# w_phi on Sync's queue, a GpSimd copy ahead of unit 1's loads, and a new table of order

## Chip, cores and metric

The kernel runs on one core of a Trainium2 chip (trn2). The metric is device time in microseconds (us) for one execution. Before the change three runs took 286.98, 287.28 and 287.29 us, median 287.28.

## What is computed

A linear attention whose feature map is a pair of exponentials, and behind it a feed-forward layer with a maximum over three projections. Its inputs are q, k, v of 8 batches x 8 heads x 576 positions x 64, `w_phi` of 64x128, and four weights of the feed-forward layer.

```python
def phi(x):
    proj = einsum('bhsd,df->bhsf', x, w_phi)
    proj = proj - max(abs(proj), axis=-1)
    return concatenate([exp(proj), exp(-proj)], axis=-1)
q_p, k_p = phi(q), phi(k)
kv  = einsum('bhsf,bhsd->bhfd', k_p, v);  z = sum(k_p, axis=2)
x   = einsum('bhsf,bhfd->bhsd', q_p, kv) / (einsum('bhsf,bhf->bhs', q_p, z) + 1e-6)
h   = maximum(maximum(x @ w1, x @ w2), x @ w3)     # x as 4608 x 512
out = h @ w_out
```

## The kernel before, in words

The attention is cut into 16 units of 4 heads (two pairs of heads). The feed-forward layer is cut into 9 chunks of 512 tokens; chunk b needs units 2b and 2b+1, the last chunk needs all of them.

What one unit does, with the names that the trace shows (lines of the kernel before):

- Load. Units 0 to 3 go by TensorE transposes (`by_pe`). Unit 0's q and k come as four float32 pieces on Sync's (SP's) queue, one piece per pair of heads (L447), and are cast to bf16 by L451 on ACT or DVE. Units 1 to 3 come on GpSimd's (POOL's) queue, cast on the way (L458). From unit 4 on, q and k come as float32 on SP or POOL (L472) and POOL casts them (L476). v is float32 in `v_raw` (L472).
- T: the transposes `tps<-ident,qk_bf`, L490 for unit 0 and L493 for units 1 to 3, evacuated by DVE into `qkT` (L496). Later units use a DMA transpose (L508).
- G: the projections `psq` and `psk` from `qkT` and `w2` (L535, L530), 18 tiles in groups of four and a last one of two. DVE takes the absolute maxima (`mqp`, `mk`, L554), ACT the exponentials of the keys (`Ek`, L548).
- M: the queries once more, the other way round, with the maxima subtracted: `psm` by L616 and L619 for units 0 and 1 (this needs all of the unit's `mqp`, and the tile `minus`), by L614 later, where the maxima reach `qkT` through a small DMA `qkT<-mT` (L570). ACT takes `Eq` from it (L627).
- V and K: POOL multiplies v with `em` into `vab` (L589); K, the sum over positions, is `kvps` (L643, 72 matmuls).
- N and x: the numerators and denominators `psn` (L661), divided by DVE (L667, L668) into `x_sb`, and turned into `xT` (L681, L684, or the DMA transpose L691).

A chunk then runs the products `ups` (L714), their maximum (`hT`, L720 to L724), the products into `ops` (L742, L747), the copy into `osb` (L755) and the store (L762). While the attention of the first units runs, the weights are turned and multiplied (`pwT` L797, `pm` L811) and subtracted on POOL (L785).

What sets the order: every piece of work is a node with a number, its engine may be one of several, and a table of words (`PLAN`) gives for each node the engine, the buffer slots and a start by which the nodes are sorted. Each engine runs its instructions strictly in that order; semaphores do the waiting. Only the sequence counts on the chip: an instruction whose input is late holds all that stands behind it on its engine. `fill` puts matmuls on a constant tile (`idler`, L842) into gaps that the table leaves on TensorE in the first part of the program; they only keep TensorE busy.

Around the change: `w_phi` comes as two DMAs of 64 rows on ACT's queue (L360) ahead of ACT's table load, and DVE casts it in three pieces (L405, L406) before the first `qkT` copy (L496). The v loads of units 1, 2 and 3 are held back by a one-element copy on DVE (L467) that reads a unit's `qkT` and writes into the tile to be loaded. TensorE starts with 17 idlers.

## Time and profile before

The profiled execution took 285.3 us from its first to its last instruction; the page shows no other time of that execution. The median of the runs is 287.28 us, so 1.98 us lie around the span.

| what | before |
|---|---|
| median of 3 runs | 287.28 us |
| profiled execution, its span | 285.3 us |
| busy: TensorE matmul, DVE, ACT, POOL | 274.8, 208.4, 192.5, 125.0 us |
| idlers (L842), 28 of them | 9.5 us of TensorE's busy time |
| first matmul that is work (`tps` L490) | at 6.50 us |
| first `ups` of a chunk | at 42.86 us |
| last copy before the last store | at 281.95 us |
| chain that ended last | PE 81%, DMA 8%, ACT 6% |

How to read it: TensorE is shown busy nearly throughout, but at the start a part of that is idlers, and a busy share there says nothing of progress. Rows of the timeline give start, length, engine, line, operation and, in brackets, how long the engine had been idle before it and what ended that. Rows of the windows view give a stretch, its length and each engine's busy time in it.

### The profile page before, as it was taken

The page shows a single profiled execution, that of the slowest core. Times are in us where ns is not written, and L with a number is a line of the kernel's source. Part 1 is how long each engine was busy: PE and PEld are TensorE (multiplying, and loading weights), DVE is VectorE, ACT ScalarE, POOL GpSimd, SP SyncE. Part 2 cuts the span into 40 slices and gives each one's busy share as a digit, 9 for nine tenths or more (in the row PEclk, how much of TensorE's full clock was granted, in tenths as well). Part 3 has the DMA queues.
Part 4 walks back from the last instruction along what each step waited for, and adds up shares of the span by engine and source line. Part 5 has one row for each costly group of instructions (what it writes and reads, how often), then busy time and mean ns, then how long its engine had stood idle before and what let it go on. Part 6 is the DMA issues. An engine that isn't in the chain of part 4 may idle for free.

```text
span 285.3 us, 8441 instructions
## 1 busy us (share of the span) xinstructions
PE 274.8 (96%) x3485; PEld 155.7 (55%) x3522; DVE 208.4 (73%) x442; ACT 192.5 (67%) x445; POOL 125.0 (44%) x107
## 2 busy tenths in 40 slices
PE   8889999999999999999999999999999999999995
PEld 3557674565565555456565565555544664444442
DVE  2897899988999868688678779987975472227431
ACT  3798979997999987878868887779775400041001
POOL 9338999945923574417534950160080501000000
PEclk9997999999999999999999999999999999999999
DMA  7999979999899998988897998294420134153135
GB/s 192 203 284 262 312 144 305 341 239 250 221 293 196 225 232 280 251 156 202 258 251 272 268 199 182 99 182 81 82 62 3 27 54 90 37 110 76 37 85 173
DMA packets 67760, 51.46 MB, mean 180 GB/s; under 512 B 48778, under 2 KB 53002, under 8 KB 67722
## 3 DMA queue, kind: packets, MB, share of 16 engines
q1 hardware_dynamic: 62734, 43.38, 60.6%
q0 software_dynamic: 4576, 7.28, 12.1%
q8 instruction: 27, 0.44, 0.6%
q10 hardware_dynamic: 412, 0.28, 0.3%
q14 instruction: 11, 0.09, 0.1%
HBM read 34.67 MB, written 9.44 MB: 155 GB/s over the span
## 4 chain that ended last, share of the span: by engine, by line
PE 81%; DMA 8%; ACT 6%; POOL 1%; DVE 1%; issue 1%; ACTq 0%; POOLq 0%
PE ups L714 29%; PE ops L747 15%; PE ops L742 10%; PE psn L661 6%; PE kvps L643 6%; DMA qk_bf<-in_q_dram 5%; PE psm L614 5%; PE psq L535 4%; DMA qkT<-mT 3%; ACT Eq L627 3%; PE pm L811 2%; ACT Ek L548 2%; PE tps L493 1%; PE psq L530 1%; POOL qk_bf L458 1%
## 5 line engine op out<-in xcount | busy, mean ns | idle before, releaser
L714 PE MATMUL ups<-xT,w_bf 128*128 128x512 bf16 x415 | 101.5, 379 | 1.4 <-ACT Ek L548 0.5
L627 ACT ACTIVATE Eq<-psm 128x512 bf16<-128x512 f32 (+1 forms) x160 | 81.9, 582 | 15.6 <-PE psm L614 12.8
L589 POOL TENSOR_TENSOR vab<-v_raw,em 128x1152 bf16<-128x1152 f32 (+1 forms) x36 | 68.1, 1907 | 36.8 <-ACT em L585 27.9
L548 ACT ACTIVATE Ek<-psk 128x512 bf16<-128x512 f32 x128 | 73.5, 622 | 8.5 <-PE psk L535 5.8
L714 PEld LDWEIGHTS <-w_bf 128*128 128x128 bf16 x432 | 40.6, 98 | 45.4 <-issue 1.0
L720 DVE TENSOR_TENSOR hT<-hT,ups 128x512 bf16<-128x512 bf16 x54 | 36.4, 683 | 24.6 <-ACT hT L722 13.6
L554 DVE TENSOR_REDUCE mqp<-psq 128x4 bf16<-128x512 f32 (+1 forms) x80 | 49.0, 633 | 5.1 <-PE psk L535 2.9
L747 PE MATMUL ops<-wout_bf,hT 128*128 128x512 bf16 (+2 forms) x215 | 51.5, 373 | 0.5 <-issue 0.2
L554 DVE TENSOR_REDUCE mk<-psk 128x4 f32<-128x512 f32 x64 | 43.0, 683 | 0.7 <-PE psk L535 0.5
L747 PEld LDWEIGHTS <-hT 128*128 128x128 bf16 x222 | 21.1, 98 | 23.1
L668 DVE TENSOR_TENSOR x_sb<-psn,rden 128x320 bf16<-128x320 f32 x64 | 31.5, 492 | 2.2
L722 ACT ACTIVATE hT<-ups 128x512 bf16<-128x512 f32 x31 | 18.5, 615 | 21.1 <-PE ups L714 21.0
L755 ACT COPY osb<-ops 128x512 f32<-128x512 f32 (+2 forms) x17 | 9.6, 581 | 30.2 <-PE ops L747 12.7
L661 PEld LDWEIGHTS <-Eq 128*128 128x128 bf16 x640 | 24.9, 97 | 8.0
L755 DVE COPY osb<-ops 128x512 f32<-128x512 f32 x20 | 13.6, 689 | 20.1 <-PE ops L747 18.5
L661 PE MATMUL psn<-kv_sb,Eq 128*128 128x65 bf16 x640 | 26.8, 194 | 0.1
L742 PE MATMUL ops<-xT 128*128 128x512 bf16 x88 | 24.2, 379 | 0.4
L614 PE MATMUL psm<-qkT,wphi_m 128*128 128x512 bf16 (+1 forms) x70 | 22.3, 359 | 0.7 <-DMA qkT<-mT 0.6
L535 PE MATMUL psq<-w,qkT 64*128 64x128 bf16 x256 | 21.5, 217 | 0.5 <-DVE qkT L496 0.2
L476 POOL CAST qk_bf<-q_raw 128x1152 bf16<-128x1152 f32 x12 | 13.8, 1148 | 18.1 <-DMA q_raw<-in_q_dram 9.7
L535 PE MATMUL psk<-w,qkT 64*128 64x128 bf16 x256 | 21.3, 217 | 0.4 <-DVE mqp L554 0.4
L535 PEld LDWEIGHTS <-qkT 64*128 64x128 bf16 x512 | 14.8, 94 | 10.7 <-issue 8.1
(76 smaller groups left out, 272.6 us busy)
## 6 DMA issues: line engine op xcount, KB each, us to landing
out_dram<-osb SPq DMA_DIRECT2D x64, 128.0 KB, 2.5
v_raw<-in_v_dram SPq DMA_DIRECT2D x14, 576.0 KB
k_raw<-in_k_dram SPq DMA_DIRECT2D x11, 576.0 KB, 4.9
q_raw<-in_q_dram SPq DMA_DIRECT2D x11, 576.0 KB, 4.9
w_bf<-in_moe_w_dram POOLq DMA_DIRECT2D x3, 768.0 KB, 11.1
v_raw<-in_v_dram POOLq DMA_DIRECT2D x2, 576.0 KB, 13.7
qk_bf<-in_k_dram POOLq DMA_DIRECT2D x3, 288.0 KB, 13.4
qk_bf<-in_q_dram POOLq DMA_DIRECT2D x3, 288.0 KB, 13.6
```

The costliest lines, as they stand in the source:

```text
L535: nc.tensor.matmul(ps()[:, i, :], lhsT=cols[r, :], rhs=w2[r, c, :], start=True, stop=True)
L548: nc.scalar.activation(Ek[s]()[:, tiles_of(t0, n), :], of(1), EXP, scale=1.0 - 2.0 * s)
L554: nc.vector.tensor_reduce((mq, mk)[c]()[:, tiles_of(t0, n)], of(c), AXX, ALU.max, apply_absolute_value=True)
L589: (nc.vector if n_.eng == "DVE" else nc.gpsimd).tensor_tensor(vab()[:, g, t0:t1, 0:D], vb()[:, t0:t1, :], em()[:, g, t0:t1].unsqueeze(2).t ...
L614: nc.tensor.matmul(psm()[:, 0:w], lhsT=wphi_m, rhs=rhs, start=True, stop=True)
L627: nc.scalar.activation(Eqb()[s][:, cols], psm()[:, 0:w], EXP, scale=1.0 - 2.0 * s)
L661: nc.tensor.matmul(psn()[:, c, :], lhsT=Eqb()[g][:, t0:t0 + P], rhs=kv()[:, pr, ab, g, :], start=(g == 0), stop=(g == 1))
L668: nc.vector.tensor_tensor(x_sb()[:, pr, :, ab, :], psn()[:, :, 0:D], rden().to_broadcast([P, 5, D]), ALU.mult)
L714: nc.tensor.matmul(ups(), lhsT=w_bf[i + 1][:, ct, j * P:(j + 1) * P], rhs=tokens_of(ct), start=(ct == 0), stop=(ct == CT - 1))
L720: nc.vector.tensor_tensor(hT()[:, j, :], hT()[:, j, :], ups(), ALU.max)
L742: nc.tensor.matmul(ops_()[:, 0:width], lhsT=tile_of(ct, tt), rhs=line_w[c_i > MOVE][:, ct, cols], start=(ct == 0), stop=False)
L747: nc.tensor.matmul(ops_()[:, 0:width], lhsT=hT()[:, j, tt * P:(tt + 1) * P], rhs=wout_bf[:, j, cols], start=False, stop=(j == JT - 1))
```

## The change

1. `w_phi` is one DMA on SP's queue, whose source is read twice (a leading dimension of two with step 0), and stands between unit 0's pieces; ACT issues none.
2. The copies on DVE that held the v loads of units 1 to 3 (L467) are gone. In their place a one-element copy on POOL reads `k_raw` of unit 0 and writes into the tile that unit 1's q or k is to be loaded into, so that these two loads, and all that stands behind them on POOL, are issued only after that piece of unit 0's k is there.
3. `fill` leaves a wider margin ahead of a matmul in the first 10 us; TensorE has 17 idlers instead of 28, and 9 instead of 17 at its start.
4. Some buffers are no longer named by nodes that only come before their use (G, M, K and N). This does not change what an instruction reads or writes.
5. The whole table `PLAN` is another.

```diff
-GATES = (None, (0, 0), (1, 0), (2, 0))
+HOLD = (1, 0)
...
-0G@0.7 4A@0.7 6S0@0.7 2D0@0.8 3D@1.0 10S0@1.2 1G@1.3 12S@1.6 85G0@1.9 8S@2.1 84G@2.6 1075G@3.3 158G1@4.0 5D@4.1
+0G@0.7 2D0@0.7 12S0@0.7 3D@0.8 8S0@1.1 4S@1.6 10S@2.0 6S@2.5 14S0@3.0 13A0@3.4 9D@4.5 5D@4.9 17T1@5.0 18D0@5.7 11A@5.8
...
-        while gap > (0.35 if t < WARM else 0.5) and t < n.start - 0.2:
+        while gap > (0.35 if t < WARM else 0.5) and t < n.start - (0.45 if t < 10 else 0.2):
...
-    for ab in range(2):
-        nc.scalar.dma_start(wphi_f[ab * D:(ab + 1) * D, :], w_phi)
...
-    n_phi = node("phi", 0, {"ACT": 1.2}, lambda: None, [], [], pipe=0.05, lat=2.0, dmas=2)
+    n_phi = node("phi", 0, {"SP": 1.2}, lambda: nc.sync.dma_start(wphi_f, w_phi.unsqueeze(0).to_broadcast([2, D, DF])), [], [],
+                 pipe=0.05, lat=2.0)
...
+                        if (what, i) == HOLD:
+                            first.append((n_.deps[0], raw))
...
+                    held = []
+                    if u == 1:
+                        land, src = first[0]
+                        held.append(nd("gate", {"POOL": 0.1}, lambda what=what, src=src: nc.gpsimd.tensor_copy(
+                            qk()[0:1, what, 0, 0:1], src()[0:1, 0, 0:1]), [land], [src, qk]))
...
-                if by_pe and u < len(GATES) and GATES[u]:
-                    src, col = units[GATES[u][0]]["qkT"], BATCHES[GATES[u][1]][0] * P
-                    gates.append(nd("gate", {"DVE": 0.1}, lambda src=src, col=col, raw=raw: nc.vector.tensor_copy(
-                        raw()[0:1, 0, 0:1], src()[0:1, col:col + 1]), [], [src, raw]))
```

Three places show what the table does at the start. First SP, from its first load on, before the change:

```order
L447 DMA q_raw<-in_q_dram 128x576
L447 DMA k_raw<-in_k_dram 128x576 x2
L447 DMA q_raw<-in_q_dram 128x576
L472 DMA v_raw<-in_v_dram 128x2x576 x2
L570 DMA qkT<-mT 1x18x128
```

SP at the same place with the change:

```order
L441 DMA k_raw<-in_k_dram 128x576
L441 DMA q_raw<-in_q_dram 128x576
L407 DMA wphi_f<-in_w_phi_dram 128x1x128
L441 DMA k_raw<-in_k_dram 128x576
L441 DMA q_raw<-in_q_dram 128x576
L468 DMA v_raw<-in_v_dram 128x2x576
L563 DMA qkT<-mT 1x18x128
```

`w_phi` now stands third, ahead of the second pieces of k and q; unit 0's v is the sixth load, where it stood on POOL's queue before, and the two held v loads of later units are gone from SP's start.

Second POOL, from the identity tile on, before the change (the DMA rows are loads that POOL issues; `qk_bf` of units 1 and 2, then v of unit 0 and two weights):

```order
masks.py:199 AFFINE_SELECT ident<-ident 128x128
L409 TENSOR_SCALAR minus<-ident 128x128
L458 DMA qk_bf<-in_k_dram 128x2x576
L458 DMA qk_bf<-in_q_dram 128x2x576
L419 DMA w_bf<-in_moe_w_dram 128x4x768
L458 DMA qk_bf<-in_k_dram 128x2x576
L458 DMA qk_bf<-in_q_dram 128x2x576
L472 DMA v_raw<-in_v_dram 128x2x576
L419 DMA wout_bf<-in_moe_w_out_dram 128x6x512
L419 DMA w_bf<-in_moe_w_dram 128x4x768
```

POOL at the same place with the change:

```order
masks.py:199 AFFINE_SELECT ident<-ident 128x128
L458 CAST qk_bf<-k_raw 1x1 x2
L454 DMA qk_bf<-in_q_dram 128x2x576
L454 DMA qk_bf<-in_k_dram 128x2x576
L413 DMA w_bf<-in_moe_w_dram 128x4x768
L454 DMA qk_bf<-in_q_dram 128x2x576
L402 TENSOR_SCALAR minus<-ident 128x128
L454 DMA qk_bf<-in_k_dram 128x2x576
L468 DMA v_raw<-in_v_dram 128x2x576
L413 DMA wout_bf<-in_moe_w_out_dram 128x6x512
L413 DMA w_bf<-in_moe_w_dram 128x4x768
L582 TENSOR_TENSOR vab<-v_raw,em 128x9x64 x2
```

The two copies of one element stand ahead of every load; the copies wait for unit 0's second piece of k, the fourth DMA on SP. `minus` has moved behind four loads, the v in this list is unit 1's, and the first two products `vab` follow the last load.

Third ACT, from the last casts or exponentials of unit 0's keys on, before the change (`Ek_208` and `Ek_222` are unit 0's two halves, `Eq_0` its queries):

```order
L548 ACTIVATE Ek_208<-psk 128x512 x2
L548 ACTIVATE Ek_222<-psk 128x512
L548 ACTIVATE Ek_208<-psq 128x2x128
L627 ACTIVATE Eq_0_75<-psm 128x512
L627 ACTIVATE Eq_0_76<-psm 128x512
L548 ACTIVATE Ek_222<-psq 128x2x128
```

ACT with the change (`Ek_172` and `Ek_211` are unit 0's, `Ek_330` and `Ek_347` unit 1's):

```order
L541 ACTIVATE Ek_172<-psk 128x512
L578 ACTIVATE em<-mk 128x9 x2
L541 ACTIVATE Ek_211<-psq 128x2x128
L541 ACTIVATE Ek_211<-psk 128x512
L620 ACTIVATE Eq_0_73<-psm 128x512
L620 ACTIVATE Eq_0_74<-psm 128x512
L541 ACTIVATE Ek_330<-psk 128x512
L541 ACTIVATE Ek_347<-psk 128x512
```

All ten exponentials of unit 0's keys and two of `em` now stand ahead of the first `Eq`. On TensorE the first `psm` that it reads has moved too: with the change it stands behind the first half of unit 1's transposes (16 matmuls, L489), and unit 0's projections all stand ahead of these.

309 lines of the change are left out of this document (151 added, 158 removed).

## The prediction

> **What bounds the kernel now.** I read the page's busy line first, then the windows by stage, then the timeline of the start.
>
> ```profile
> PE 274.8 (96%) x3485; PEld 155.7 (55%) x3522; DVE 208.4 (73%) x442; ACT 192.5 (67%) x445; POOL 125.0 (44%) x107
> L842 PE MATMUL idler<-idle 128*128 128x512 bf16 x28 | 9.5, 462 | 1.0 <-DVE idle L412 1.0
> ```
>
> TensorE is busy for 274.8 of 285.3 us, but 9.5 us of it are idlers. The stretches say where it is really the bound (columns: length; busy time of PE, PEld, DVE, ACT, POOL; granted clock; share of the DMA engines; GB/s):
>
> ```profile
> 10.00:24.00 14.00, 12.33 (x197) 8.83 (x199) 13.23 (x28) 12.77 (x32) 6.41 (x9) 0.91 1.17 247
> 24.00:43.00 19.00, 18.75 (x411) 13.72 (x412) 16.48 (x40) 16.67 (x43) 17.69 (x15) 0.98 0.97 242
> 43.00:60.00 17.00, 16.90 (x206) 9.18 (x207) 16.61 (x33) 16.93 (x40) 16.95 (x11) 1.00 1.05 301
> 60.00:110.00 50.00, 49.14 (x802) 29.19 (x810) 43.52 (x96) 45.08 (x108) 24.82 (x17) 1.00 1.00 241
> 110.00:180.00 70.00, 68.50 (x964) 39.31 (x968) 56.56 (x119) 56.48 (x133) 34.30 (x26) 1.00 0.90 233
> 180.00:282.00 102.00, 101.24 (x883) 52.20 (x891) 58.15 (x115) 40.10 (x90) 17.18 (x16) 1.00 0.35 76
> ```
>
> From 43 us on TensorE idles 0.10 + 0.86 + 1.50 + 0.76 = 3.22 us in 239: it is the bound, and a new order can win at most about that. Between 10 and 43 us DVE and ACT are as full as TensorE (ACT idles 1.23 + 2.33 = 3.56 us, DVE 0.77 + 2.52), the DMA engines are full too, and TensorE fills up with idlers. So the head goes at the pace of ACT's and DVE's streams, and what counts is when they start and where they stop. Their start:
>
> ```profile
> 0.73 1.25 ACTq L360 DMA_DIRECT2D wphi_f<-in_w_phi_dram  x2
> 0.73 0.40 SPq L447 DMA_DIRECT2D q_raw<-in_q_dram  x1
> 1.04 5.52 PE L842 MATMUL idler<-idle 128*128 128x512 bf16 x17 [1.04 <-DVE idle L412]
> 3.53 0.67 ACT L451 CAST qk_bf<-q_raw 128x576 bf16<-128x576 f32 x1 [0.24 <-DMA q_raw<-in_q_dram]
> 4.64 0.67 ACT L451 CAST qk_bf<-k_raw 128x576 bf16<-128x576 f32 x1 [0.44 <-DMA k_raw<-in_k_dram]
> 6.11 0.41 DVE L405 CAST w<-wphi_f 64x128 bf16<-64x128 f32 x1 [2.14 <-DMA wphi_f<-in_w_phi_dram]
> 6.50 0.61 PE L490 MATMUL tps<-ident,qk_bf 128*128 128x128 bf16 x8
> 6.54 0.22 DVE L406 CAST wphi_m<-wphi_f 64x128 bf16<-64x128 f32 x1
> 7.14 0.69 DVE L496 COPY qkT<-tps 128x1024 bf16<-128x1024 bf16 x1 [0.39 <-PE tps L490]
> 7.64 0.67 ACT L451 CAST qk_bf<-k_raw 128x576 bf16<-128x576 f32 x1 [2.33 <-DMA k_raw<-in_k_dram]
> 7.89 0.23 PE L535 MATMUL psq<-w,qkT 64*128 64x128 bf16 x1
> 9.29 0.67 ACT L451 CAST qk_bf<-q_raw 128x576 bf16<-128x576 f32 x1 [0.98 <-DMA q_raw<-in_q_dram]
> 9.87 4.14 ACT L548 ACTIVATE Ek<-psk 128x512 bf16<-128x512 f32 x8
> 12.07 1.24 PE L493 MATMUL tps<-ident,qk_bf 128*64 128x128 bf16 x32
> 13.47 0.38 PE L616 MATMUL psm<-qkT,w 128*128 128x512 bf16 x1
> 13.87 0.42 ACT L548 ACTIVATE Ek<-psq 128x256 bf16<-128x256 f32 x1
> 14.13 1.13 ACT L627 ACTIVATE Eq<-psm 128x512 bf16<-128x512 f32 x2
> 15.44 3.08 ACT L627 ACTIVATE Eq<-psm 128x512 bf16<-128x512 f32 x6
> ```
>
> The four pieces of unit 0 land at 3.53, 4.64, 7.64 and 9.29 us: 1.11 us apart at first, later 3.0 and 1.65, since other loads share the engines. The first projection is at 7.89 us, and ACT's stream of exponentials begins at 9.87 us, once it has cast the last piece; unit 1 is transposed at 12.07 us.
>
> **The change part by part.** The sum is made against the span of 285.3 us; the median of the runs, 287.28 us, is 1.98 us more, and I add the difference in span to it.
>
> *Fewer idlers.* Seventeen ended at 1.04 + 5.52 = 6.56 us and held the first transposes, whose casts were done at 4.64 + 0.67 = 5.31 us. At the 0.43 us from one to the next at which they begin, nine end by 4.9. That frees up to 1.2 us, but the first projection needs `w_phi` as well, so its landing decides.
>
> *w_phi between the pieces.* What it costs there is the largest unknown. ACT's queue is q10 on the page:
>
> ```profile
> q10 hardware_dynamic: 412, 0.28, 0.3%
> ```
>
> 0.3% of 16 engines for 285.3 us is 13.7 us of one engine for 412 packets, 33 ns each. The 128 rows of `w_phi` are 4.3 us of one engine: 0.27 us if 16 engines share them, 4.3 if one has them all, and what stands behind them on those engines waits for that. The source counts 2 x 64 x 128, and I take two engines, 2.1 us. Behind the second piece (4.64) this puts `w_phi` at some 6.4 us, between 6.7 and the 6.11 at which its second half landed before, and so much later than its size suggests.
> The Trainium skill has a rule that speaks against this edit ("DMA: Bandwidth & Descriptors", the section on why a DMA increments its semaphore by 16): the number of engines is the largest up to 16 that divides the slowest dimension of both sides, so a leading broadcast of two would leave two engines. No row here shows that for this DMA; by it the term is my 2.1 us, and without it 0.27.
>
> With `w_phi` at 6.4, DVE's three casts (0.41 + 0.22 + less than 0.41, partly overlapped, 0.65 as between 6.11 and 6.76) end at 7.05, the copy of `qkT` at 7.7, and the first projection is at about 7.75 instead of 7.89. The second k lands a piece later, 6.4 + 1.1 = 7.5 (before 7.64), the second q at 8.6 (9.29): nothing else competes by then. ACT's stream begins behind its cast at 9.25 instead of 9.87, 0.6 earlier. It gains nothing else: the first q's cast has gone to DVE, where 0.68 us of an f32 copy lies in the wait for `w_phi`, and the 1.25 us of issuing on ACT lay ahead of a table load that nothing waited for.
>
> *The hold.* Two copies of one element, then the loads.
>
> ```profile
> L467 DVE CAST v_raw<-qkT 1x1 f32<-1x1 bf16 x3 | 0.4, 134 | 0.0
> 1.90 0.94 POOL L458 DMA_DIRECT2D qk_bf<-in_k_dram  x1
> 9.72 0.72 POOL L472 DMA_DIRECT2D k_raw<-in_k_dram  x1 [1.65 <-DMA qk_bf<-in_k_dram]
> 11.12 0.73 POOL L472 DMA_DIRECT2D q_raw<-in_q_dram  x1 [0.68 <-DMA qk_bf<-in_q_dram]
> 18.41 0.51 ACT L585 ACTIVATE em<-mk 128x9 f32<-128x9 f32 x4
> 20.46 4.49 POOL L589 TENSOR_TENSOR vab<-v_raw,em 128x576 bf16<-128x576 f32 x4 [1.21 <-DMA v_raw<-in_v_dram]
> 26.09 1.27 PE L643 MATMUL kvps<-vab,Ek 64*128 64x65 bf16 x72
> 42.86 2.54 PE L714 MATMUL ups<-xT,w_bf 128*128 128x512 bf16 x11
> ```
>
> A copy takes 0.13 us on DVE; on POOL I take 0.3 for both. So unit 1's first load is issued at 7.5 + 0.3 = 7.8 us instead of 1.90, and behind it on POOL wait two weights, unit 2's q and k, `minus` (needed with the first `psm`, long after) and unit 1's v. Before, the two landed by 9.72 and 11.12, 7.8 and 9.2 us after that first issue, against unit 0's pieces. Now only v of unit 0 is in their way. Lower bound: the issue 0.94, the 1.7 us that a piece on SP takes beside its own 1.1 (0.73 to 3.53), and twice the 1.40 from 9.72 to 11.12: 5.4 us, 13.2. Upper bound: 9.2 us again, 17.0. I take 14.5, nearer to the lower end since the pieces are gone: 2.4 us after 12.07.
>
> What waits for that: TensorE runs unit 1's first transposes ahead of unit 0's first `psm`. ACT has, from 9.25 on, eight exponentials (4.14), two short ones of 0.42 and two `em` of 0.51 / 4, 5.25 us, to 14.5. The first `Eq` can start at 14.5 + 0.62 (half of the 1.24) + 0.66 (a `psm` at 13.47, its `Eq` at 14.13), 15.8: ACT stops for 1.3 us. Before, the same content without the two `Eq` that stood among it was done by 15.44 - 1.13 + 0.26 = 14.6. So the head is 1.2 us behind at this place.
>
> *Given back later.* Unit 0's v is now the sixth load on SP, 8.6 + 2 x 1.1 = 10.8 us, instead of the release at 20.46; POOL can multiply as soon as its issues end, at about 14.5. K of unit 0 (26.09 us before), the numerators and unit 0's x follow earlier, and with them there is work for ACT and DVE where ACT idled 2.33 us between 24 and 43 us. I count all of that: 1.2 - 2.3 = -1.1 for the head, the first `ups` at 41.8. Ends: -3.5 (no stop, all idling gone) and +2.5 (a long stop, little regained).
>
> *The rest of the table.* From 43 us on 3.22 us can be won, and a bad order can lose as much. One row shows what an order does:
>
> ```profile
> 112.22 1.54 ACTq L570 DMA_DIRECT2D qkT<-mT  x1
> ```
>
> The small DMA of the maxima, issued by ACT, held ACT's queue for 1.54 us; three of four such issues move to SP. I take a third of the bound, -1.1, ends -3.2 and +2. At the end the last copy moves from ACT (0.48 us at 281.95) to DVE, within 0.2; nothing.
>
> ```profile
> 281.95 0.48 ACT L755 COPY osb<-ops 128x384 f32<-128x384 f32 x1 [1.40 <-PE ops L747]
> ```
>
> Sum: -1.1 - 1.1 = -2.2 us, a span of 283.1 and a time of **285.1 us**.
>
> **The rivals.**
>
> *w_phi costs nothing* (0.27 us): it lands by 4.9, k at 6.0, q at 7.1; ACT starts at 7.75, 2.1 earlier, unit 1 lands at 13.0, and ACT stops from 13.0 to 14.3: a lead of 1.6 at the stop, of 0.3 behind it. Then -0.3 - 2.3 for the head and -1.1 for the rest: 283.6 us. For it: 64 KB are little. Against: the row at 6.11.
>
> *Unit 1 is too late* (the other side): the loads take their 9.2 us again and land at 17.0. ACT then stops from 14.5 to 18.3, 2.5 us more than forecast, and TensorE, which has two idlers there, stands for over 4 us. What that does, the trace shows once (columns: length, PE busy, clock, DMA, GB/s):
>
> ```profile
> 21.00:22.00 1.00, 0.74 (x12) 0.77 1.20 237
> 22.00:23.00 1.00, 1.00 (x8) 0.50 1.24 209
> 24.00:25.00 1.00, 1.00 (x18) 0.53 1.19 221
> ```
>
> The clock was at 0.5 for some 3.4 us (0.46 of the first row's microsecond, two whole ones, 0.94 of the last), which costs up to 1.7 us of matmuls. Together 2.5 + 1.7 = 4.2 on the forecast: 289.3 us. It turns to slower from a landing at 16.7 on, or from 15.0 if the clock falls.
> The Trainium skill ("TensorE: Matmul & The Clock Gate", Part 1) has the gate at half rate after an idle window of about 3.4 us, for at least as long; the 3.4 us agree. By it the stop that the forecast leaves TensorE, some 3 us with two idlers in it, is at the edge: -2.2 would become about -0.5.
>
> *The rest pays it back*: the head wins 1.1, but later units' loads, held behind the first ones, bring new waits on SP or POOL, and TensorE idles 1.1 us more after 43: 287.3 us, no change. The same comes out if the hold does nothing, because the DMA engines are full (1.17) either way.
>
> **How the numbers follow.** Forecast 0.40 (its own range 283.9 to 286.7), w_phi for nothing 0.25 (282.3 to 283.9), unit 1 too late 0.20 (287.9 to 290.5), paid back 0.15 (286.7 to 287.9). The range leaves out a tenth on each side: 282.3 to 288.9. A measurement of this kernel can tell about 0.2%, 0.57 us, from no change. Faster by more: 0.40 + 0.25 and little of the rest, 0.65; the same 0.12; slower 0.23.
>
> **What would show it.** `w_phi`'s cast on DVE: near 5 us, the first rival; near 6.5, the forecast. ACT's first exponential at 9.3. Unit 1's first transposes at 14.5, and the clock in the 4 us behind them. `kvps` of unit 0 ahead of its 26.09 us. The first `ups` at 41.8 instead of 42.86. TensorE's idle time from there to the last 5 us: 2.1 instead of 3.22. The prediction is wrong if the first `ups` is later than 43, or if the rest idles more than now.

## The result and the profile after

The change made the kernel slower: **289.69 us** (median of 4 runs, 288.99 to 290.24) against 287.13 us of the kernel before on the same chip (286.77 to 287.29), a ratio of 1.0097 [1.0069, 1.0125]. Twelve more runs on another chip, one of the experiments below, gave 1.0078 [1.0045, 1.0111]. The forecast was 285.1 us, its range ended at 288.9, and "unit 1 is too late" had been priced at 289.3. The ratios leave out disturbed runs, those over 1.5% above the fastest run of the same kernel.

The busy line of the changed kernel's page:

```profile
PE 272.6 (95%) x3474; PEld 154.6 (54%) x3511; DVE 202.2 (70%) x427; ACT 196.9 (68%) x454; POOL 126.1 (44%) x112
```

Without its idlers TensorE was busy for 274.8 - 9.5 = 265.3 us; now it is 272.6 - 6.7 = 265.9 us (the 17 idlers of this trace take 6.7), in a span that is 2.8 us longer. So the work is about the same, and the time has gone into waiting. The stretches of the changed kernel, with the columns of the prediction's table, say where:

```profile
10.00:24.00 14.00, 11.17 (x189) 8.28 (x191) 11.49 (x24) 11.30 (x29) 12.80 (x18) 0.88 1.14 211
24.00:43.00 19.00, 17.31 (x408) 12.86 (x406) 16.29 (x38) 16.69 (x44) 14.45 (x12) 1.00 1.00 230
43.00:60.00 17.00, 16.84 (x191) 9.03 (x191) 16.16 (x30) 16.39 (x38) 15.90 (x11) 1.00 0.87 239
60.00:110.00 50.00, 47.59 (x733) 28.23 (x739) 42.95 (x97) 43.92 (x104) 29.28 (x21) 1.00 1.10 253
110.00:180.00 70.00, 68.56 (x1027) 39.77 (x1037) 55.04 (x114) 57.91 (x138) 32.76 (x25) 1.00 0.95 221
180.00:282.00 102.00, 101.26 (x882) 52.23 (x893) 55.02 (x111) 45.66 (x101) 17.65 (x17) 1.00 0.41 89
```

From 10 to 24 us ACT now idles 2.70 us where it idled 1.23, and from 24 to 43 us 2.31 where it idled 2.33: the idle time that I meant to regain is all still there, and TensorE idles 1.69 us in that stretch where it idled 0.25. From 60 to 110 us TensorE idles 2.41 us instead of 0.86 (both traces lack 37 matmul records, so both are somewhat high).

The timeline of the start holds the rows that the prediction named (start, length, and in brackets the idle time ahead and what ended it):

```profile
1.63 0.72 SPq L407 DMA_DIRECT2D wphi_f<-in_w_phi_dram  x1
3.64 0.67 ACT L445 CAST qk_bf<-k_raw 128x576 bf16<-128x576 f32 x1 [1.64 <-DMA k_raw<-in_k_dram]
6.55 0.46 DVE L398 CAST w<-wphi_f 64x128 bf16<-64x128 f32 x2 [1.47 <-DMA wphi_f<-in_w_phi_dram]
7.19 0.67 ACT L445 CAST qk_bf<-k_raw 128x576 bf16<-128x576 f32 x1 [2.88 <-DMA k_raw<-in_k_dram]
7.22 0.30 POOL L458 CAST qk_bf<-k_raw 1x1 bf16<-1x1 f32 x2 [5.93 <-DMA k_raw<-in_k_dram]
9.07 2.74 ACT L541 ACTIVATE Ek<-psk 128x512 bf16<-128x512 f32 x5 [0.47 <-DVE mk L547]
15.06 0.61 PE L489 MATMUL tps<-ident,qk_bf 128*64 128x128 bf16 x15 [2.24 <-DMA qk_bf<-in_k_dram]
16.34 1.09 ACT L620 ACTIVATE Eq<-psm 128x512 bf16<-128x512 f32 x2 [1.92 <-PE psm L612]
43.02 3.63 PE L707 MATMUL ups<-xT,w_bf 128*128 128x512 bf16 x15
```

`w_phi` is cast at 6.55 us (6.4 forecast), ACT's stream starts at 9.07 (9.25), the two holding copies take 0.30 us together, as assumed. Unit 1's transposes start in bulk at 15.06 (14.5), and ACT stops for 1.92 us (1.3) until the first `Eq` at 16.34 (15.8). Up to here the forecast is half a microsecond off. Then it parts from the trace: the first `ups` comes at 43.02 instead of 41.8.

The chain of work that ended last, followed back to its start, ties these rows together (its longer pieces; start and length):

```profile
1.63 0.72 SPq L407
2.40 4.77 DMA k_raw<-in_k_dram
7.22 0.31 POOL qk_bf L458 x2
7.71 0.89 POOL qk_bf L454
8.60 6.33 DMA qk_bf<-in_k_dram
15.06 0.61 PE tps L489 x15
```

Unit 0's second piece of k is issued behind `w_phi` and lands at 7.17 us. That releases the two holding copies; unit 1's k is issued from 8.60 us on and is there at 14.93, and TensorE, idle for 2.24 us, goes on at 15.06. So `w_phi`, the hold and unit 1 stand behind each other on one chain, and from there on the chain runs on TensorE, which is busy for 8.94 of the next 9 us.

Behind unit 1's late landing the granted clock (third column from the end) fell to half, as that rival had it:

```profile
16.00:17.00 1.00, 1.00 (x24) 0.91 (x20) 1.00 (x2) 0.66 (x2) 1.00 (x2) 0.50 1.15 209
17.00:18.00 1.00, 1.00 (x22) 0.83 (x18) 0.13 (x1) 0.52 (x2) 1.00 (x2) 0.50 1.15 201
18.00:19.00 1.00, 1.00 (x12) 0.36 (x7) 1.00 (x2) 1.00 (x4) 0.11 (x1) 0.50 1.24 218
```

It was 0.79 in the next microsecond, so the drop lasted some 3.4 us. The Trainium skill's window of about 3.4 us ("TensorE: Matmul & The Clock Gate", Part 1) agrees with that length. TensorE's longest idle stretch ahead of the drop was shorter, 2.24 us.

### The profile page after: what moved, and what is told of

It reads as the page before. It is cut to its first block, busy times and chain, and to the rows that moved or that the text cites. A ratio compares the mean times of both kernels' runs of the same rounds, so it can differ in the third digit from the quotient of the medians.

```text
span 288.1 us, 8410 instructions
## 1 busy us (share of the span) xinstructions
PE 272.6 (95%) x3474; PEld 154.6 (54%) x3511; DVE 202.2 (70%) x427; ACT 196.9 (68%) x454; POOL 126.1 (44%) x112
## 4 chain that ended last, share of the span: by engine, by line
PE 80%; DMA 13%; ACT 2%; issue 2%; DVE 1%; SPq 1%; POOL 0%; ACTq 0%; DVEq 0%
PE ups L707 29%; PE ops L740 13%; PE ops L735 9%; DMA qkT<-mT 7%; PE psn L654 6%; PE kvps L636 6%; PE psm L607 5%; PE psq L528 4%; DMA qk_bf<-in_k_dram 2%; PE pm L804 2%; DMA out_dram<-osb 2%; DMA k_raw<-in_k_dram 2%; PE tps L489 1%; ACT Eq L620 1%; PE psq L523 1%
## 5 line engine op out<-in xcount | busy, mean ns | idle before, releaser
L582 POOL TENSOR_TENSOR vab<-v_raw,em 128x1152 bf16<-128x1152 f32 (+1 forms) x36 | 68.2, 1910 | 40.7 <-ACT em L578 35.2
L541 ACT ACTIVATE Ek<-psk 128x512 bf16<-128x512 f32 x128 | 72.7, 620 | 5.5 <-PE psk L528 3.2
L740 PE MATMUL ops<-wout_bf,hT 128*128 128x512 bf16 (+2 forms) x212 | 49.7, 373 | 0.8 <-issue 0.5
L713 DVE TENSOR_TENSOR hT<-hT,ups 128x512 bf16<-128x512 bf16 x54 | 35.7, 680 | 19.9 <-PE ups L707 10.7
L715 ACT ACTIVATE hT<-ups 128x512 bf16<-128x512 f32 x36 | 21.6, 615 | 33.0 <-PE ups L707 32.9
L740 PEld LDWEIGHTS <-hT 128*128 128x128 bf16 x222 | 20.5, 98 | 22.1
L654 PE MATMUL psn<-kv_sb,Eq 128*128 128x65 bf16 x640 | 27.5, 194 | 1.1 <-issue 1.1
L748 ACT COPY osb<-ops 128x512 f32<-128x512 f32 (+1 forms) x20 | 11.5, 576 | 22.9 <-PE ops L740 17.3
L748 DVE COPY osb<-ops 128x512 f32<-128x512 f32 (+1 forms) x17 | 11.5, 679 | 21.8 <-PE ops L740 20.5
L472 POOL CAST qk_bf<-k_raw 128x1152 bf16<-128x1152 f32 x12 | 13.7, 1145 | 21.4 <-DMA k_raw<-in_k_dram 10.1
L636 PE MATMUL kvps<-vab,Ek 64*128 64x65 bf16 x1152 | 20.4, 190 | 0.5 <-issue 0.4
## 6 DMA issues: line engine op xcount, KB each, us to landing
v_raw<-in_v_dram POOLq DMA_DIRECT2D x2, 576.0 KB, 14.4
```

Source lines behind the costliest of these rows:

```text
L541: nc.scalar.activation(Ek[s]()[:, tiles_of(t0, n), :], of(1), EXP, scale=1.0 - 2.0 * s)
L582: (nc.vector if n_.eng == "DVE" else nc.gpsimd).tensor_tensor(vab()[:, g, t0:t1, 0:D], vb()[:, t0:t1, :], em()[:, g, t0:t1].unsqueeze(2).t ...
L636: nc.tensor.matmul(kvps[ab]()[:, t // NT, g, :], lhsT=Ek[g]()[r, t, :], rhs=vab()[r, g, t, :], start=(t + g == 0), stop=(t == UT - 1 and g ...
L654: nc.tensor.matmul(psn()[:, c, :], lhsT=Eqb()[g][:, t0:t0 + P], rhs=kv()[:, pr, ab, g, :], start=(g == 0), stop=(g == 1))
L713: nc.vector.tensor_tensor(hT()[:, j, :], hT()[:, j, :], ups(), ALU.max)
L740: nc.tensor.matmul(ops_()[:, 0:width], lhsT=hT()[:, j, tt * P:(tt + 1) * P], rhs=wout_bf[:, j, cols], start=False, stop=(j == JT - 1))
```

## The experiments

The theory after this result: unit 1's late landing costs the head, and the form in which `w_phi` is loaded is what makes it late. Its rivals: the clock drop is what costs; the first `psm` behind unit 1's transposes is what costs; or the head is harmless, and the new order of the rest costs, by its waits for the maxima's small DMAs or by its shape. All ratios are against the kernel before on the same chip.

### The two kernels again

Kernel before, unchanged:

> The kernel before once more, for a trace with all its TensorE records. Theory T (the new order behind 40 us costs 1.6 us by itself): against the run with the old head and the new rest, as much work left at 43 us (within 0.5), and 1 to 1.6 us less from 180 us on. If instead it already has 1 us less at 43 us, that difference was made in the head, where the two stand in the same order.

286.69 us, span 284.9. Its first `ups` and its stretches:

```profile
41.38 2.75 PE L714 MATMUL ups<-xT,w_bf 128*128 128x512 bf16 x12
10.00:24.00 14.00, 12.69 (x224) 9.23 (x223) 14.00 (x30) 13.57 (x35) 7.65 (x10) 1.00 1.17 248
24.00:43.00 19.00, 18.80 (x393) 13.06 (x392) 17.20 (x42) 16.68 (x43) 17.70 (x14) 1.00 1.03 253
43.00:60.00 17.00, 17.00 (x226) 9.20 (x225) 16.60 (x33) 16.93 (x42) 15.66 (x11) 1.00 1.00 300
60.00:110.00 50.00, 49.42 (x818) 29.23 (x811) 43.30 (x96) 44.85 (x109) 24.80 (x17) 1.00 1.03 238
110.00:180.00 70.00, 68.56 (x951) 38.88 (x950) 55.90 (x118) 55.83 (x129) 34.26 (x26) 1.00 0.92 232
180.00:282.00 102.00, 101.45 (x884) 51.90 (x882) 57.73 (x114) 40.07 (x89) 17.16 (x16) 1.00 0.35 76
```

The same program reached its first `ups` at 41.38 us here, not at 42.86. Its granted clock is 1.00 from 10 us on, and ACT is busy 13.57 us between 10 and 24, where it was 12.77. The trace that the prediction was made from is level with this one up to 21 us and 1.2 us behind at 25, so it lost about a microsecond around the clock drop quoted there, in the same order. Three further traces that have before's order in the head (three experiments below) show the first `ups` at 41.05, 41.49 and 41.72 us: 42.86 is the odd one. I had planned to win back what a run without the drop does not lose.

The change, unchanged:

> The changed kernel once more, beside the others on one chip, and with a trace that has all its TensorE records (35 are missing from the first). If the first result holds: 1.007 to 1.0125 of before. TensorE's work left at 43 us: 1.0 to 1.5 us more than in the run with w_phi as two plain DMAs, and 2 us more at the end.

1.0078 [1.0045, 1.0111]; 12 runs from 287.05 to 292.44 us. The profiled one took 287.92 (span 286.1), with `w_phi` cast at 7.10 us, unit 1's transposes in bulk at 15.91 and its first `ups` at 43.18.

With a trace of before that has no clock drop there is a better measure than one row. For each trace I counted the work that TensorE still has ahead of it at a given time: all matmuls but the idlers that start later, each at its form's full-clock duration (0.216 us for 512 columns, 0.016 for 65; where a trace lacks a few records of a form, the others make up for them). The difference to before's second trace says how far a kernel is behind there.

| us behind before's second trace | at 15 us | at 25 us | at 43 us | at the end (span) | from 43 us on | TensorE's waits from 43 us on |
|---|---|---|---|---|---|---|
| before, first trace | 0.0 | 1.2 | 1.5 | 0.4 | -1.1 | 1.3 |
| before, second trace | 0 | 0 | 0 | 0 | 0 | 1.9 |
| change, first trace | 2.6 | 1.1 | 2.0 | 3.2 | +1.2 | 3.0 |
| change again | 2.6 | 1.2 | 2.0 | 1.2 | -0.8 | 1.2 |
| w_phi_two_plain | 1.2 | -0.2 | 0.9 | 1.1 | +0.2 | 1.2 |
| two_plain_again | 1.5 | 0.3 | 1.0 | 1.9 | +0.9 | 3.5 |
| w_phi_on_ACT | 0.3 | -1.0 | 0.2 | 0.1 | -0.1 | 1.6 |
| w_phi_on_ACT_no_hold | 1.6 | 0.1 | 0.7 | 3.5 | +2.8 | 4.2 |
| two_plain_no_hold | 2.7 | 1.5 | 2.3 | 3.9 | +1.6 | 3.4 |
| no_hold | 4.1 | 6.7 | 6.4 | 5.7 | -0.7 | 1.9 |
| head_old_rest_new | 0.0 | 0.3 | 0.7 | 1.1 | +0.4 | 1.6 |
| psm_first | -0.1 | 1.3 | 2.1 | 3.1 | +1.0 | 1.9 |
| psm_first_w_phi_on_ACT | 1.4 | 2.3 | 2.6 | 3.4 | +0.8 | 2.2 |

Read it in two parts. The head (at 43 us) is 2.0 us behind in both traces of the change, whatever their totals. The rest goes from -0.8 to +2.8 in kernels that share the new order, and mostly as TensorE's waits in the last column go (the sum of its rows in the view of waits). Two traces of one program differ there by 1.1 (before) and 2.0 us (the change), so a single entry says little. Four traces lack 37 records each (both first ones, two_plain_again, two_plain_no_hold), so their middle columns are the less exact. The first column is the least sure of all: its 2.6 comes out when each of unit 1's waiting transposes counts for 0.055 us; at the 0.028 us at which the traces run them back to back, both traces of the change are 1.6 us behind at 15 us.

### How w_phi is loaded

Two plain DMAs at the same place on SP, nothing else changed:

```diff
-    n_phi = node("phi", 0, {"SP": 1.2}, lambda: nc.sync.dma_start(wphi_f, w_phi.unsqueeze(0).to_broadcast([2, D, DF])), [], [],
+    n_phi = node("phi", 0, {"SP": 1.2}, lambda: [nc.sync.dma_start(wphi_f[ab * D:(ab + 1) * D, :], w_phi) for ab in range(2)], [], [],
```

> The changed kernel with w_phi on SP at the same place, but as two DMAs of 64 rows without the leading dimension of two. Theory E (the one DMA with a leading dimension of two runs on two engines only, and what stands behind it on them waits): DVE's cast of w_phi starts at 5.2 to 5.8 us instead of 6.55, the second k's cast near 6.5 instead of 7.19, and the time is 0.5 to 1.5 us less than that of the change, 1.004 to 1.008 of before. Rival (the place on the queue counts, not the form): the cast stays at 6.3 to 6.6 us and the time at 1.009 to 1.011.

1.0038 [1.0006, 1.007]. In its timeline `w_phi` is issued twice, 0.47 us more of SP's time than one issue, and is there earlier:

```profile
1.64 1.19 SPq L407 DMA_DIRECT2D wphi_f<-in_w_phi_dram  x2
5.48 0.46 DVE L398 CAST w<-wphi_f 64x128 bf16<-64x128 f32 x2 [0.35 <-DMA wphi_f<-in_w_phi_dram]
42.11 3.63 PE L707 MATMUL ups<-xT,w_bf 128*128 128x512 bf16 x16
```

The cast comes 1.07 us earlier, unit 1's transposes 1.30 (13.76), the first `ups` 0.91. Repeated on another chip:

> The run with w_phi as two plain DMAs and the hold, once more. If its first result holds: w_phi cast near 5.5 us, 0.5 to 1.2 us more work left for TensorE at 43 us than in before, a time of 1.001 to 1.007. If the first was luck: 1.008 to 1.011, as the change.

1.0042 [1.0008, 1.0076], cast at 5.49, first `ups` at 42.05. So of the 0.8 to 1.0% that the change costs, the form of this one DMA is 0.4 to 0.6%, 1.0 to 1.7 us. Each ratio is known to some 0.3%, so the sign is clearer than the size.

The packets show what the form does. The traces keep start and length of every DMA packet, and the 128 packets of 512 bytes at the start are `w_phi`'s rows. In six of the seven traces with the one DMA they start two every 24 ns, and in the seventh (no_hold, below) two every 124 ns; never are more than four under way at once. In all thirteen traces with two plain DMAs, on either queue, up to seven to ten are under way at once. That is what a load on two engines would look like; the records do not name the engine.

Back on ACT's queue as two DMAs, the rest of the change kept:

```diff
+    for ab in range(2):
+        nc.scalar.dma_start(wphi_f[ab * D:(ab + 1) * D, :], w_phi)
...
-    n_phi = node("phi", 0, {"SP": 1.2}, lambda: nc.sync.dma_start(wphi_f, w_phi.unsqueeze(0).to_broadcast([2, D, DF])), [], [],
+    n_phi = node("phi", 0, {"SP": 1.2}, lambda: None, [], [],
```

> The changed kernel with w_phi as two DMAs of 64 rows on ACT's queue, as before, instead of one on SP between the pieces. Theories T and D: w_phi lands by about 6.1 instead of 6.55 us and the last pieces up to 2 us earlier, no change beyond 0.6 us: 289 to 290.3 us. Theory W (w_phi on SP delays the pieces behind it, and this is the loss): 287 to 288 us.

1.0041 [1.0006, 1.0077]: the cast is at 5.54 and the first `ups` at 41.32, level with before. The time is no better than with two plain DMAs on SP, although the head is 0.7 us better in the traces; intervals of 0.35% cannot tell 0.7 us. With a head that is level the kernel is still 0.1 to 0.8% slower, so the order of the rest costs something, by little more than its noise.

The old kernel with the one DMA third on SP's queue:

```diff
-    for ab in range(2):
-        nc.scalar.dma_start(wphi_f[ab * D:(ab + 1) * D, :], w_phi)
...
-    n_phi = node("phi", 0, {"ACT": 1.2}, lambda: None, [], [], pipe=0.05, lat=2.0, dmas=2)
+    n_phi = node("phi", 0, {"SP": 1.2}, lambda: nc.sync.dma_start(wphi_f, w_phi.unsqueeze(0).to_broadcast([2, D, DF])), [], [], pipe=0.05, lat=2.0)
```

> The kernel before, its own order and no hold, with w_phi as the one DMA on SP between the pieces (third on SP). With nothing held, the changed kernel had its w_phi cast at 12.63 us. Theory E: the same happens here, the cast is at 10 to 13 us instead of 6.11, the first projection 4 to 6 us later than 7.89, and the time 3 to 6 us more (1.010 to 1.021). Rival (w_phi is 64 KB, and its place on the queue makes no difference): within 1 us, 1.000 to 1.003.

Six runs fell into two groups: 285.81 and 286.77 us, and four from 293.47 to 294.82. The trace is that of 286.77, with `w_phi` cast at 6.44 and the first `ups` at 41.49. The runs agree too little for a ratio, and what divides the groups stays open: in the old order, too, `w_phi` at 6.44 costs nothing in some runs. What the trace does show is that the one DMA can land that early beside GpSimd's loads, which nothing held here (the first was issued at 1.90 us).

### The hold

The change without it: the two copies read the identity tile, which is there early, so unit 1's loads go out at once.

```diff
-                            qk()[0:1, what, 0, 0:1], src()[0:1, 0, 0:1]), [land], [src, qk]))
+                            qk()[0:1, what, 0, 0:1], ident[0:1, 0:1]), [land], [src, qk]))
```

> The changed kernel, but the two one-element copies on GpSimd read the identity tile, which is there at once, so that nothing holds unit 1's loads. Theory D: the DMA engines are full from 3 us on again, and the time falls to 286.5 to 287.8 us. Theory T: unit 0's pieces land as late as before, the head is no better, and the order behind costs the same: 289 to 290.5 us.

1.0232 [1.0194, 1.0269]. DVE waited 7.57 us for `w_phi`:

```profile
12.63 0.46 DVE L398 CAST w<-wphi_f 64x128 bf16<-64x128 f32 x2 [7.57 <-DMA wphi_f<-in_w_phi_dram]
47.24 2.12 PE L707 MATMUL ups<-xT,w_bf 128*128 128x512 bf16 x9
```

With the same edit and `w_phi` as two plain DMAs:

> The changed kernel with nothing held and w_phi on SP as two plain DMAs of 64 rows. With the one DMA and nothing held, w_phi was cast at 12.63 us, and the time was 1.023. Theory E (the form: few engines, behind unit 1's loads on each): now the cast is at 5.5 to 7.5 us, unit 1 at 13 to 15, the time 1.004 to 1.010. Rival (any DMA of SP is late beside GpSimd's loads): the cast at 10 to 13 us, the time 1.018 to 1.025.

1.0117 [1.0069, 1.0165].

```profile
5.50 0.22 DVE L398 CAST w<-wphi_f 64x128 bf16<-64x128 f32 x1 [0.39 <-DMA wphi_f<-in_w_phi_dram]
6.21 0.23 DVE L398 CAST w<-wphi_f 64x128 bf16<-64x128 f32 x1 [0.49 <-DMA wphi_f<-in_w_phi_dram]
43.46 3.63 PE L707 MATMUL ups<-xT,w_bf 128*128 128x512 bf16 x15
```

That pair is the clearest of the study: with GpSimd's loads under way the one DMA is cast at 12.63 us, the halves of the two plain ones at 5.50 and 6.21. The packets agree: `w_phi`'s 128 rows take from 3.88 to 12.14 us as one DMA, two every 124 ns, and from 3.58 to 5.79 as two. It need not come so (old_with_w_phi_on_SP had 6.44), and why it did here and not there stays open. Without the hold the pieces behind `w_phi` land late even with two plain DMAs (second k and q cast at 8.51 and 10.64). So with `w_phi` on SP the hold is worth some 2 us (1.0117 against 1.0038 and 1.0042). And with `w_phi` on ACT:

```diff
+    for ab in range(2):
+        nc.scalar.dma_start(wphi_f[ab * D:(ab + 1) * D, :], w_phi)
...
-                            qk()[0:1, what, 0, 0:1], src()[0:1, 0, 0:1]), [land], [src, qk]))
+                            qk()[0:1, what, 0, 0:1], ident[0:1, 0:1]), [land], [src, qk]))
```

> The changed kernel with w_phi on ACT's queue and nothing held (the two copies read the identity tile). With w_phi on SP, no hold cost 3 us more, since w_phi then landed at 12.6 us. Theory E (the hold is needed only because of w_phi's form): w_phi lands by 6.2 us, unit 1 earlier than 13.2, and the time is that of w_phi on ACT with the hold or less, 1.000 to 1.005 of before. Rival (the new order needs the early pieces of unit 0, whatever w_phi does): 1.008 to 1.015.

1.0054 [1.0026, 1.0083], beside 1.0041 with the hold: no difference that these intervals tell. Its head is 0.7 us behind, not 0.2. In the old kernel the hold was tried alone, by two copies of one element on POOL ahead of unit 1's loads that read unit 0's second piece of k:

```diff
+                        if u == 1:
+                            nc.gpsimd.tensor_copy(qk()[0:1, what, 0, 0:1], raws[0][1]()[0:1, NT, 0:1])
```

> The kernel before, its own order, w_phi on ACT, with only the hold: two one-element copies on GpSimd ahead of unit 1's loads that wait for the third piece on SP. Theory D (what is not loaded in the first microseconds is missing later, since the DMA engines are full from 5 to 40 us): unit 0's last pieces land up to 2 us earlier, but unit 1's and all that stands behind come 4 to 6 us later than in before, and the order of before waits for them: 1 to 4 us slower, 1.004 to 1.014. Rival (earlier pieces move ACT's stream, and the hold costs nothing): 0.5 to 1.5 us faster, 0.995 to 0.998.

1.0139 [1.0091, 1.0186]. The old order, made for early loads of unit 1, pays 4 us for having them late. Its trace, of a run of 469.16 us at a granted clock of 0.56, is not used. Here the hold alone is a loss; a gain was seen only in the new order with `w_phi` on SP.

### Unit 1, the first psm and the clock

If the stop of ACT at 14.4 us were what costs, putting three of unit 0's `psm` and six `Eq` ahead of unit 1's first transposes should cure it. In the table (first changed row; the idlers as they were):

```diff
-27A@10.2 24D@10.4 41T3@10.6 1077G@10.9 42A@11.0 29D@11.0 23A@11.2 45D@11.6 89T5@11.7 22A@11.7 1075G@11.7 44D@11.9
+27A@10.2 24D@10.4 41T3@10.6 1077G@10.9 42A@11.0 29D@11.0 23A@11.2 45D@11.6 22A@11.7 1075G@11.7 44D@11.9 54T2@11.9
...
```

> The changed kernel with three of unit 0's psm (and their six Eq on ACT) ahead of unit 1's first transposes on TensorE, instead of behind them. Theory Q (the loss of the head is the queue: psm could start at 13.5 us, when unit 0's last maxima are there, and stand until 15.6 behind transposes that wait for unit 1): the first Eq starts near 14.5 instead of 16.34 to 17.11 us, ACT's stop of 1.9 us is gone, TensorE's work left at 43 us is 0 to 1 us more than that of before instead of 2.0, and the time 1 to 2 us less than that of the change: 1.003 to 1.007 of before. Rival (unit 1's late landing costs the same, whatever stands ahead: ACT runs out of work a little later): 1.8 to 2.2 us at 43 us, 1.008 to 1.011.

1.0134 [1.0096, 1.0172]. The stop is gone, and a later one has come:

```profile
14.02 3.07 ACT L624 ACTIVATE Eq<-psm 128x512 bf16<-128x512 f32 x6
20.39 0.38 ACT L624 ACTIVATE Eq<-psm 128x256 bf16<-128x256 f32 x1 [1.65 <-PE psm L616]
43.30 3.63 PE L711 MATMUL ups<-xT,w_bf 128*128 128x512 bf16 x16
```

The first `Eq` moved from 16.34 to 14.02, and the first `ups` from 43.02 to 43.30. In the table above it is level with before at 15 us, and 2.1 behind at 43: ACT had been given its work earlier, and ran out of it later. That speaks against the rival that the first `psm` is what costs. The head goes with `kvps` of unit 1 instead, as that tile's rows of the changed kernel, of before's second trace and of w_phi_on_ACT show (144 matmuls of units 0 and 1, first to last start):

```profile
L636 PE MATMUL kvps<-vab,Ek x144: 187/190/202, 24.1 to 34.9; 64*128 64x65 bf16 x144
```

```profile
L643 PE MATMUL kvps<-vab,Ek x144: 187/190/201, 24.4 to 32.7; 64*128 64x65 bf16 x144
```

```profile
L638 PE MATMUL kvps<-vab,Ek x144: 187/190/203, 21.9 to 33.2; 64*128 64x65 bf16 x144
```

| kernel | unit 1's transposes in bulk | last `kvps` | first `ups` | between the two |
|---|---|---|---|---|
| w_phi_on_ACT | 13.19 | 33.2 | 41.32 | 8.1 |
| w_phi_two_plain | 13.76 | 34.0 | 42.11 | 8.1 |
| psm_first | 14.26 | 35.2 | 43.30 | 8.1 |
| change | 15.06 | 34.9 | 43.02 | 8.1 |
| psm_first_w_phi_on_ACT | 15.16 | 36.0 | 44.09 | 8.1 |
| two_plain_no_hold | 15.83 | 35.3 | 43.46 | 8.1 |
| change again | 15.91 | 35.1 | 43.18 | 8.1 |
| no_hold | 21.35 | 39.1 | 47.24 | 8.1 |

In the new order the first `ups` stands 8.1 us behind unit 1's last `kvps` in all fourteen traces that have its head, and that stands 18.8 to 21.2 us behind unit 1's transposes, except in no_hold (17.8), where unit 0 is late as well. So the head ends with a chain through unit 1, and the later unit 1 lands, the later the head mostly ends; the second distance varies by 2 us, and no edit moved unit 1's landing alone.

The same with `w_phi` on ACT:

> The same with w_phi on ACT's queue. There the first Eq began at 14.39 us, and TensorE had 0.22 us more left at 43 us than in before. Theory Q: the first Eq near 13.3, 0.5 to 1 us less left at 43 us than in before, 0.999 to 1.004. Rival: as with w_phi on ACT alone, 1.004 to 1.0075.

1.0101 [1.0071, 1.013], worse than w_phi_on_ACT alone; its first `ups` is at 44.09. Unit 1's transposes, behind the moved `psm`, start at 15.16 instead of 13.19.

On the clock: among the change's runs whose mean granted clock was 1.000 throughout (287.05, 287.32, 288.98, 289.84, 290.24; mean 288.69) and the eight others that count in its ratios (mean 289.25), the difference is 0.56 us. The runs of the two groups spread over 3 and 2 us, so that does not price the drop; the 1.7 that I had priced is not excluded. But the runs without a drop are still 1.6 us above 287.13, the higher of before's two medians, and in the trace of change_again the drop lies at 8.5 to 11.9 us with a head as late as in the other. So it is not the main cause.

### The rest of the table

Three hybrids of the two orders. The change's code and rows up to 40 us, before's order behind:

```diff
-104D1@15.2 96A@15.2 160G2@15.5 1086T7@15.7 65A@15.7 94D@15.8 98D@16.0 62A@16.2 115T1@16.2 48G@16.2 66T4@16.4 1087D0@16.6
+104D1@15.2 96A@15.2 160G2@15.5 1086T7@15.7 65A@15.7 94D@15.8 98D@16.0 62A@16.2 115T1@16.2 48G@16.2 66T4@16.4
...
```

> The changed kernel's code and its order up to 40 us of the table; behind that the order of before. TensorE has the same work left at 43 us in both traces, and the loss of 2.6 us comes after that. Theory T (the new table's order behind 40 us is the worse one: it gives the small DMA of the maxima too little time, or puts it behind more on SP's queue): 286.5 to 287.5 us, the order of before repairs it. Theory D (a debt: the held loads leave the DMA engines idle at the start, 0.68 of their time from 5 to 10 us where before had 1.08, what was not loaded then is loaded later, and late DMAs are paid by whatever order follows): 289 to 290 us.

1.0519 [1.0476, 1.0563]. Before's code and rows up to 40 us, the change's order behind:

```diff
-153T5@40.1 156A@40.3 236T112311@40.4 154D@40.5 241T46@40.7 198A@40.8 235D@40.9 251T07@40.9 242A@41.1 244D@41.1
+153T5@40.0 154A@40.0 236T112311@40.0 235D@40.0 251T64@40.0 156D@40.0 241T05@40.0 198A@40.0 253A@40.0 254D@40.0
...
```

> The reverse: the code of before and its order up to 40 us of its table, and behind that the new table's order. Theory T: 289 to 290 us, as slow as the whole change. Theory D: 286.5 to 287.5 us, since no debt is made. Between the two (288 to 288.8) both carry a part.

1.0063 [1.0043, 1.0084], with a head 0.7 us behind at 43 us. Before's up to 75 us, the change's behind:

```diff
-1147T5@73.8 329A1@73.8 435D@73.9 415A@74.0 330G1@74.2 443A@74.3 444D@74.5 1159T6@74.6 432A@74.8 1148D0@75.1 452A@75.3
+1147T5@73.8 329A1@73.8 435D@73.9 415A@74.0 330G1@74.2 443A@74.3 444D@74.5 1159T6@74.6 432A@74.8 427S3@75.0 331G@75.0
...
```

> The order of before up to 75 us of its table, the new one behind. With the seam at 40 us it was 1.0063. If the loss of that run is made between 40 and 75: 0.999 to 1.002. If behind 75 us: 1.004 to 1.008.

1.0332 [1.0295, 1.0369]; one wait of a `psm` for a copy on DVE at the seam takes 5.4 us. Two of the three are misses as experiments: what a seam costs (9 to 15 us) hides what was asked. The middle one says at least that the new order behind an old head, seam included, loses 0.6%, and wins nothing.

Next the maxima. In the changed kernel's first trace TensorE waits for their small DMAs more often than in before's second (waits of TensorE from 43 us on; total, times, longest; in the change's second trace it is 0.7 us, once). Two of these DMAs in the first trace's chain of work that ended last took this long from issue to landing (the longest in the chains of before's two traces took 5.33 and 5.19):

```profile
PE psm L607 <- DMA qkT<-mT: 1.9, 4, 0.7
```

```profile
PE psm L614 <- DMA qkT<-mT: 1.4, 2, 0.9
```

```profile
75.33 4.65 DMA qkT<-mT
90.95 6.37 DMA qkT<-mT
```

Of fourteen such issues ACT had four before and has one now; SP has thirteen. Four of them, of units 4, 6, 8 and 13, given to ACT (first changed row):

```diff
-399A@67.3 412T05@67.7 408A@67.8 326D1@67.8 1138D3@67.9 327S@68.0 328A1@68.2 407A@68.4 330G1@68.6 430T43@68.8 684S0@69.0
+399A@67.3 412T05@67.7 408A@67.8 326D1@67.8 1138D3@67.9 327A@68.0 328A1@68.2 407A@68.4 330G1@68.6 430T43@68.8 684S0@69.0
...
```

> The changed kernel with the small DMA of the maxima of units 4, 6, 8 and 13 issued by ACT instead of SP; nothing else. In the change they left SP at 75.33, 90.95, 102.58 and 156.55 us and landed 4.65, 6.37, 3.60 and 5.56 us later. Theory Q (they queue behind loads and transposes on SP's own queue): they land within 3.5 us, TensorE's waits for them fall from 1.9 us to under 0.7, and the time is 0.8 to 1.5 us less than that of the change, 1.0045 to 1.007 of before. Rival (the DMA engines are full, whatever the queue; and ACT pays for the issue): no change, 1.009 to 1.012.

1.0171 [1.0126, 1.0216], worse by 0.7 to 0.9%. The wait stayed, and ACT, which issues them now, is waited for as well (same view):

```profile
PE psm L607 <- DMA qkT<-mT: 1.7, 2, 1.0
PE psn L654 <- issue: 1.1, 1, 1.1
PE ups L707 <- ACT Eq L620: 0.9, 1, 0.9
```

One of the four, issued by ACT at 91.67 us, took 6.66 us to land, so SP's queue is not what makes them late. If they only need more time, the `psm` of units 4, 6, 7, 8, 10 and 13 may stand 1.2 us later in the table, and ACT's work on them with it (one of its entries; `w_phi` on ACT, the idlers as they were):

```diff
-344T2@73.1
+344T2@74.3
...
```

> The changed kernel with w_phi on ACT, and the psm of units 4, 6, 7, 8, 10 and 13 set 1.2 us later in TensorE's order, so that their maxima have longer to land. Theory L (late landings of the maxima are what the rest of the new order loses): TensorE's waits for them, 1.1 us in that run and 3.1 in the one without hold, fall under 0.5, the time to 1.000 to 1.003 of before with half the spread. Rival (ACT, which reads psm, then waits instead): no change, 1.004 to 1.008.

1.0322 [1.0298, 1.0345].

```profile
PE psn L660 <- ACT Eq L626: 2.2, 2, 1.2
PE kvps L642 <- ACT Eq L626: 1.7, 2, 1.5
PE psk L534 <- ACT Eq L626: 1.6, 3, 0.8
```

The wait for the DMA went down to 0.4 us, and TensorE waits for ACT's exponentials instead, which the later `psm` now holds up: 8 us worse than w_phi_on_ACT. Both table edits together:

> Both orders of psm and w_phi on ACT together. If theories Q and L hold: 0.995 to 1.001 of before, the only version of the new order that could beat it. If neither holds: 1.004 to 1.008.

1.0375 [1.0353, 1.0396], the sum of the two losses over w_phi_on_ACT within their intervals.

The traces hint at the place of the rest's loss, and no edit cured it. Where the new order's traces lose most behind 43 us (w_phi_on_ACT_no_hold, +2.8), these are the waits:

```profile
PE psm L609 <- DMA qkT<-mT: 3.1, 3, 1.4
PE psm L609 <- ACT osb L750: 1.1, 1, 1.1
```

Where they lose nothing (change_again, -0.8) the first of them is 0.7. That is a loose relation, argued and not shown by an edit: no_hold waits 1.9 us for these DMAs and loses nothing behind 43 us, and two_plain_again waits 0.6 and loses 0.9. What costs in the rest stays open.

## Why the prediction was wrong

- **w_phi's term was right.** Forecast 6.4 us, measured 6.55 and 7.10 in the two traces; two plain DMAs at the same place 5.48. The first rival (it costs nothing) fails at its first condition. The Trainium skill's rule for the number of engines ("DMA: Bandwidth & Descriptors", the section on why a DMA increments its semaphore by 16) agrees with the packets: never more than four of the one DMA's under way at once, against seven to ten of the two plain ones. No record here names the engines themselves.
- **The start of the streams was right**: first exponential 9.07 (9.25). POOL's first products of unit 0 begin at 14.39 (14.5).
- **The hold's price was half a microsecond too small, in the second trace 1.4**: 15.06 and 15.91 for 14.5, ACT's stop 1.92 for 1.3. It lies between my bounds and is not by itself what turned the sign.
- **"Given back later" is the step that failed.** I counted that earlier products and earlier k of unit 0 would fill all of the 2.33 us that ACT idled between 24 and 43 us. ACT idles 2.31 there now. TensorE was at most 2.6 us behind at 15 us and still 2.0 at 43, so at most 0.6 us came back instead of 2.3, and from 25 to 43 us it fell back by another 0.9. ACT was not the engine to ask: from 24 to 43 us TensorE had been busy for 18.75 of 19.00 us in the trace that I read, with only two idlers (0.78 us) in it, so about 1.0 us was all that could come back on TensorE. My reading that TensorE fills up with idlers between 10 and 43 us did not hold there. Unit 0's first `kvps` came at 24.1 (24.4 in before's second trace), but unit 1's last at 34.9 instead of 32.7, and the head ends 8.1 us behind that. I followed the unit that the change hastens, and not the one that it holds. What a version with the new head is behind at 15 us it is, within 0.9, behind at 43 as well, unless its `psm` were moved or nothing was held with the one DMA.
- **The trace that I started from had a clock drop** from 21.5 to 24.9 us, and its 42.86 was late for that; the second trace (41.38) has none. Of "the first `ups` at 41.8 instead of 42.86" the kernel before does more by itself. I had quoted that drop as a sample of what a stop costs, and not asked whether it belonged to the kernel. Against the first trace the change's first one would be 0.5 us behind at 43 us and lose 2.3 after it, so the split into head and rest hangs on which trace of before is taken as usual.
- **The rest failed as well: forecast -1.1, measured about +0.7**, the mean of the table's eleven rows with the new order (-0.8 to +2.8; the change's own two are +1.2 and -0.8). The 3.22 us that I called winnable were too many: the first trace lacks 37 records of 3522, whose gaps may look like idle time, and the full second trace idles 0 + 0.58 + 1.44 + 0.55 = 2.57 us. The "third of the bound" rested on one row of an issue on ACT, and moving such issues either way gave nothing.
- **Which rival came**: "unit 1 is too late", at 289.3 us. Its landing at 15.06 with the clock down lies just past the point it named (15.0 if the clock falls). Its place and its sign held. Its pricing only partly: the stop was 0.6 us longer than forecast and not 2.5, what the clock cost was not resolved, and what filled the sum was the idle time not given back and the rest of the table. That its 289.3 lies so near 289.69 is luck.

The account: 2.0 us in the head (about 1.0 by `w_phi`'s form, since two plain DMAs leave 0.9 to 1.0; most of the other 1.0 by `w_phi` standing ahead of unit 0's second pieces on SP, since on ACT 0.2 is left) and some 0.7 us in the rest make 2.7, where the medians differ by 2.6 and 3.0. The head's part is shown by edits; the 0.7 is a mean over traces of several kernels, and its cause is open. With `w_phi` on ACT the hold stays and the head is level, so the hold costs the head little by itself: it passes on what delays unit 0's second k.

No version tried beats the kernel before; the best with the new order are the three with `w_phi` as two plain DMAs, at 1.0038 to 1.0042.

## What to carry to other kernels

Before a change is credited with filling idle time, name the chain that ends the stage, and ask which of the moved loads lies on it: hastening unit 0 while holding unit 1 moves nothing if the stage ends with unit 1. Idle time of one engine can be won only as far as the busiest engine of that stretch has room. Take a second trace of the kernel before, and look at its granted clock by the microsecond, before any of its stretches is called winnable. A small load that much waits for did better here as two plain DMAs of 64 rows than as one DMA with a leading dimension of two.
